# Single-bank PSUM pools for the expert products of an attention and MoE kernel

## The chip, the cores and the metric

One core of one Trainium2 chip. The metric is the device time of the program in microseconds. The kernel before took 519.79 us, the median of three runs (519.32 to 521.63).

## What is computed

Attention over q, k, v (4 batches, 8 heads, 768 positions, 64 wide), each position looking at a window of 16 and at sums of blocks of 32, gives 3072 rows x of 512. Each row then goes to one of eight experts:

```python
logits = x @ w_gate
e_idx = np.argmax(logits, axis=1)
...
for e in range(E):
    mask = e_idx == e
    ...
    h = np.maximum(x[mask] @ w1[e], 0.0)
    ye = h @ w2[e]
    out[mask] = gate_w[mask, None] * eom[mask, e, None] * ye
```

w1 is 8 x 512 x 1024, w2 is 8 x 1024 x 512, all in fp32.

## The kernel before

`body` computes the attention first, head group by head group, with the routing between. The rows of an expert are then worked off in items of up to 256 tokens, and a half item has up to 128. fp32 products are made of two halves of each operand: `split_w` (L885, L886) makes a weight's high half on ACT and its low half on DVE out of a raw tile that SP's queue loads; `take_x` (L888 to L901) transposes the gathered tokens on TensorE (L898) and splits them into xh (ACT, L900) and xl (DVE, L901).

A wide item (`full`) has eight first products (`first_wide`, L924), one for each 128 of the 1024 hidden columns: each is four pairs of matmuls (L932, L934) into one PSUM bank. Its bank is read by ACT (L936) and DVE (L937), which make lo; out of lo come hh (relu on ACT, L938) and hl (DVE, L939). The second products (`second_block`, L1115 to L1117, called Y below) multiply hh and hl with w2's halves into two banks, 48 matmuls for an item, six for each hidden tile. `write` scales the result on DVE and ACT and scatters it by an indirect DMA of POOL (L1140). `fetch` gathers the tokens of a later item (POOL, L847), `fetch_list` the rows of its list (L832). Item 1 (`full_with`) has another form of first product (`first`, twelve matmuls of 256 columns, L916 to L918); its bank is read by ACT (hh, L919) and DVE (hl, L920) themselves. During item 1 DVE also computes the routing tables of the rest (L642 to L690 and L728 to L760).

PSUM has eight banks here: tags S, PT and PV have a pair of banks each, a tile of two banks (`bank_pair`), and TR and MS one each. `Experts.bank` gives the products their banks: for S, PT and PV the first call takes one pair tile, and then its two halves go out in turn. First products alternate between PT (even) and S (odd), Y uses PV. A wait for a tile is a wait for the readers of the whole tile.

What sets the order: up to and including item 1 the order on all engines is written by hand. Items 2 to 8 (`run`) are straight code in which only POOL's order is written, and a scheduler orders PE, ACT, DVE and SP by the dependencies. After them come branches (`rest`, `pairs`, L1158): on this input three pairs of a full item and a half item run, scheduled in the same way, the half item's PE, ACT and DVE by hand. In a half item the first products are matmuls of 512 hidden columns (L1067 to L1069) into S, relu on ACT makes h (L1075), and `turn` transposes h into PT (L1080).

```python
def bank(self, tag):
    if tag not in PAIRS:
        return self.ps.tile([P, 512], F32, name="bank", tag=tag, bufs=1)
    if tag not in self.halves:
        pair = bank_pair(self.ps, tag, f"own{tag}")
        self.halves[tag] = itertools.cycle((pair[:, 0], pair[:, 1]))
    return next(self.halves[tag])
```

Of the kernel before, what the change touches and what calls it, by code (L numbers as in the profile page):

```python
# [11 lines left out]
F32 = mybir.dt.float32  # L12
# [6 lines left out]
PSUM = bass.MemoryType.PSUM  # L19
DRAM = bass.MemoryType.DRAM  # L20

B, H, S, D = 4, 8, 768, 64
P = 128
# [8 lines left out]
PAIRS = ("S", "PT", "PV")  # L32
# [137 lines left out]
def body(tc, q, k, v, w_gate, w_ogate, w1, w2, ident, cst, out):  # L170
    nc = tc.nc
    with (
        tc.tile_pool(name="const", bufs=1, side="left") as const,
        tc.tile_pool(name="ps", bufs=2, space=PSUM) as ps,
        tc.tile_pool(name="dr", bufs=1, space=DRAM) as dr,
        tc.tile_pool(name="tail", bufs=1, side="right") as st,
    ):
        id_sb = const.tile([P, P], F32, name="id_sb")
        nc.sync.dma_start(id_sb, ident)
        c_sb = const.tile([P, C_TRI], F32, name="c_sb")  # L180
        nc.gpsimd.dma_start(c_sb, cst[:, 0:C_TRI])
        wg_sb = const.tile([P, NC, 32], F32, name="wg_sb")
        nc.gpsimd.memset(wg_sb, 0.0)
        nc.gpsimd.dma_start(wg_sb[:, :, 0:E], w_gate.rearrange("(c p) e -> p c e", p=P))
        nc.gpsimd.dma_start(wg_sb[:, :, E:2 * E], w_ogate.rearrange("(c p) e -> p c e", p=P))
        x_dr = dr.tile([N, DM], F32, name="x_dr")
        l_dr = dr.tile([E * N + P, LROW], I32, name="l_dr")

        pool_a = tc.tile_pool(name="early", bufs=1, side="left")
        pool_b = tc.tile_pool(name="late", bufs=1, side="right")  # L190
        sa, sb = pool_a.__enter__(), pool_b.__enter__()
        rt = route_setup(tc, const, sa, ps, c_sb, cst, l_dr)
        moe = Experts(tc, const, ps, w1, w2, id_sb, x_dr, l_dr, rt, out)
        with tc.manual_schedule(engines=ALL):
            made = early_slots(tc, const, c_sb, rt)

            def table():
                slots = next(made)
                if slots is not None:
                    moe.add_slots(slots)  # L200

            def begin():
                pool_a.__exit__(None, None, None)
                moe.open_first(tc.tile_pool(name="moe1", bufs=2, side="left", reuse_waits="tile"))
                moe.start()

            def swap():
                pool_b.__exit__(None, None, None)
                moe.open_second(tc.tile_pool(name="moe2", bufs=2, side="right", reuse_waits="tile"))
                moe.loads = RAWS  # L210
                moe.load_ahead()

            scatters = attention(tc, const, sa, sb, st, ps, dr, q, k, v, id_sb, c_sb, wg_sb, x_dr, l_dr, rt, moe, table,
                                 begin, swap)
            counts = moe.full_with(1, scatters, rest_slots(tc, const, c_sb, rt))
        with tc.manual_schedule(engines={mybir.EngineType.Pool}):
            moe.run()
        moe.rest(counts)
        moe.close()


def bank_pair(ps, tag, name):
    return ps.tile([P, 2, 512], F32, name=name, tag=tag, bufs=1)


def shaped(bank, shape):
    b = bank[0:shape[0], 0:math.prod(shape[1:])]
    return b if len(shape) == 2 else b.rearrange("p (a n) -> p a n", n=shape[2])


def route_setup(tc, const, sa, ps, c_sb, cst, l_dr):
    nc = tc.nc
    r = {"scatters": []}
    r["ones"] = const.tile([P, P], BF16, name="ones")
    nc.vector.memset(r["ones"], 1.0)

    warm = bank_pair(ps, "S", "warm")
    for _ in range(WARM):
        nc.tensor.matmul(warm[:, 0, 0:P], lhsT=r["ones"], rhs=r["ones"], start=True, stop=True)
    r["tri"] = const.tile([P, P], BF16, name="tri")  # L240
    tri = sa.tile([P, P], F32, name="tri_f")
    nc.gpsimd.dma_start(tri, cst[:, C_TRI:C_END])
    nc.vector.tensor_copy(r["tri"], tri)

    r["base"] = const.tile([P, E], F32, name="base")
    nc.vector.tensor_copy(r["base"], c_sb[:, C_BASE:C_BASE + E])
    r["gap"] = const.tile([P, NT], F32, name="gap")
    fill = sa.tile([P, 16, LROW], I32, name="fill")
    nc.gpsimd.memset(fill, 0)
    nc.gpsimd.iota(fill[:, :, 0:1], pattern=[[1, 16]], base=NOLIST, channel_multiplier=16)  # L250
    r["fill"] = fill
    r["pair"] = const.tile([P, 2 * TB, LROW], I32, name="pair")
    nc.gpsimd.memset(r["pair"], 0)
    return r


def attention(tc, const, sa, sb, st, ps, dr, q, k, v, id_sb, c_sb, wg_sb, x_dr, l_dr, rt, moe, table, begin, swap):
# [72 lines left out]
    def gather_means(b):  # L330
        mg = banks["mg", b] = bank([P, P], f"mg{b}")
        for j in range(4):
            nc.tensor.matmul(mg[32 * j:32 * j + 32], lhsT=c_sb[:, C_SUM:C_SUM + 32],
                             rhs=MT[:, 2 * j:2 * j + 2, :].rearrange("p h d -> p (h d)"), start=True, stop=True)
# [132 lines left out]
    def turn_x(i):  # L467
        b, tok = tiles[i]
        xp = banks["xp", i] = bank([P, NC, P], f"xtr{b}{tok}")
        for c in range(NC):  # L470
            nc.tensor.transpose(xp[:, c, :], xss[i][:, 2 * c:2 * c + 2, :].rearrange("p h d -> p (h d)"), id_sb)
# [223 lines left out]
def early_slots(tc, const, c_sb, rt):  # L695

    nc = tc.nc
    base = c_sb[:, C_BASE:C_BASE + E]
    t = const.tile([P, E], F32, name="t_early")
    ti = const.tile([P, E], I32, name="ti_early")  # L700
    nc.vector.tensor_tensor(ti, rt["base"], base, ALU.subtract)
    yield
    nc.vector.tensor_scalar(ti, ti, 8, None, ALU.logical_shift_right)
    yield
    nc.vector.tensor_copy(t, ti)
    yield
    for x in slot_table_steps(tc, const, c_sb, "a", EARLY, t, base):
        if x is None:
            yield
    slots, inc, exc = x  # L710

    early = const.tile([P, E], F32, name="early")
    capped = const.tile([P, E], F32, name="capped")
    nc.vector.tensor_scalar(capped, exc, float(EARLY), None, ALU.min)
    yield
    nc.vector.scalar_tensor_tensor(early, inc, float(EARLY), capped, ALU.min, ALU.subtract)
    rt["early"] = early
    yield slots
# [50 lines left out]
class Experts:  # L769
# [3 lines left out]
    def __init__(self, tc, const, ps, w1, w2, id_sb, x_dr, l_dr, rt, out):  # L773
        self.tc, self.const, self.ps, self.w1, self.w2 = tc, const, ps, w1, w2
        self.id_sb, self.x_dr, self.l_dr, self.rt, self.out = id_sb, x_dr, l_dr, rt, out
        self.slots, self.expert, self.raw, self.lists = {}, {}, {}, {}
        self.loads, self.at = 0, [0, 0]
        self.turn = itertools.cycle(("TR", "MS"))
        self.halves = {}
        self.ring = self.fixed(const, "lst", 6, [P, 2, LROW], I32)  # L780

    def bank(self, tag):
        if tag not in PAIRS:
            return self.ps.tile([P, 512], F32, name="bank", tag=tag, bufs=1)
        if tag not in self.halves:
            pair = bank_pair(self.ps, tag, f"own{tag}")
            self.halves[tag] = itertools.cycle((pair[:, 0], pair[:, 1]))
        return next(self.halves[tag])

    def fixed(self, pool, name, n, shape, dt):  # L790
        made = []
# [25 lines left out]
    def close(self):  # L817
        self.pool2.__exit__(None, None, None)
        self.pool1.__exit__(None, None, None)
# [399 lines left out]
```

## Time and profile before

| what | value |
|---|---|
| median of 3 runs | 519.79 us (519.32 to 521.63) |
| the profiled execution | 514.76 us, span 512.9 us, mean granted clock of TensorE 0.976 |
| TensorE (PE) busy | 476.7 us, 93% of the span |
| VectorE (DVE) busy | 386.6 us, 75% |
| ScalarE (ACT) busy | 340.3 us, 66% |
| GpSimd (POOL) busy | 222.1 us, 43% |
| moved by DMA | 222 GB/s over the span |

The span is that of the instructions of the profiled execution; the rest of its time lies around them. Attention lasts to about 190 us, item 1 and the end of the item before it to 224 us, the straight items to about 390 us, the three pairs to the end. An engine's busy time is an average over these stages.

### The profile page before, as it was taken

The page shows a single profiled execution, that of the slowest core. Times are in us where ns is not written, and L with a number is a line of the kernel's source. Part 1 is how long each engine was busy: PE and PEld are TensorE (multiplying, and loading weights), DVE is VectorE, ACT ScalarE, POOL GpSimd, SP SyncE. Part 2 cuts the span into 40 slices and gives each one's busy share as a digit, 9 for nine tenths or more (in the row PEclk, how much of TensorE's full clock was granted, in tenths as well). Part 3 has the DMA queues.
Part 4 walks back from the last instruction along what each step waited for, and adds up shares of the span by engine and source line. Part 5 has one row for each costly group of instructions (what it writes and reads, how often), then busy time and mean ns, then how long its engine had stood idle before and what let it go on. Part 6 is the DMA issues. An engine that isn't in the chain of part 4 may idle for free.

```text
span 512.9 us, 12191 instructions
## 1 busy us (share of the span) xinstructions
PE 476.7 (93%) x4166; PEld 395.7 (77%) x4166; DVE 386.6 (75%) x756; ACT 340.3 (66%) x636; POOL 222.1 (43%) x235
## 2 busy tenths in 40 slices
PE   9899989989887999899999999999997999999992
PEld 9678677776666888788888888888885877877872
DVE  1977888699682687966878777777874688797795
ACT  3587755787756664566766666776763696686783
POOL 5695632635856448644224150504233315215212
PEclk9999989999897999999999999999997999999998
DMA  9999985967554699195859494866838379589380
GB/s 237 221 252 224 224 223 132 247 195 164 143 187 158 198 390 333 45 306 186 270 158 309 143 313 151 290 192 223 260 118 286 125 231 347 162 268 372 91 289 26
DMA packets 108730, 111.38 MB, mean 217 GB/s; under 512 B 42879, under 2 KB 70111, under 8 KB 108657
## 3 DMA queue, kind: packets, MB, share of 16 engines
q1 hardware_dynamic: 100496, 93.59, 61.6%
q0 software_dynamic: 8160, 16.91, 10.1%
q8 instruction: 35, 0.57, 0.5%
q14 instruction: 39, 0.31, 0.2%
HBM read 98.71 MB, written 15.15 MB: 222 GB/s over the span
## 4 chain that ended last, share of the span: by engine, by line
PE 59%; issue 15%; DVE 12%; DMA 5%; POOL 4%; ACT 3%; SPq 2%; POOLq 0%; DVEq 0%; ACTq 0%
PE ownPV L1117 7%; PE ownPV L1116 7%; PE ownPV L1115 7%; PE ownPT L932 6%; PE ownS L932 6%; PE ownPT L934 3%; PE ownS L934 3%; DMA xg<-x_dr,lst 3%; PE bank L999 3%; PE pv L449 2%; PE pt L433 2%; PE sp L399 2%; PE bank L898 2%; DVE pr L408 2%; PE ms L324 2%
## 5 line engine op out<-in xcount | busy, mean ns | idle before, releaser
L1140 POOL DMA_INDIRECT out_dram<-y,lst x27 | 32.4, 1200 | 152.2 <-DVE y L1137 148.2
L1115 PE MATMUL ownPV<-w2h,hh 128*128 128x512 f32 x216 | 85.8, 397 | 1.2 <-ACT hh L938 1.2
L1117 PE MATMUL ownPV<-w2h,hl 128*128 128x512 f32 x216 | 85.5, 396 | 0.8 <-DVE hl L939 0.8
L1116 PE MATMUL ownPV<-w2l,hh 128*128 128x512 f32 x216 | 84.7, 392 | 0.0
L421 POOL TENSOR_TENSOR pr<-pr,mn 128x960 f32<-128x960 f32 x24 | 44.5, 1861 | 40.6 <-DVE mn L416 26.1
L886 DVE TENSOR_TENSOR w2l<-wrawb,w2h 128x512 fp32r<-128x512 f32 x80 | 53.7, 688 | 9.6 <-ACT w2h L885 9.2
L932 PE MATMUL ownPT<-xhl,w1h 128*128 128x512 f32 x160 | 59.6, 404 | 0.9 <-issue 0.9
L932 PE MATMUL ownS<-xhl,w1h 128*128 128x512 f32 x160 | 60.0, 406 | 0.0
L885 ACT ACTIVATE w2h<-wrawb 128x512 fp32r<-128x512 f32 x80 | 48.6, 630 | 11.5 <-PE ownPV L1117 11.0
L847 POOL DMA_INDIRECT xg<-x_dr,lst x34 | 37.9, 1115 | 39.6 <-PE bank L898 11.9
L886 DVE TENSOR_TENSOR w1l<-wrawb,w1h 128x512 fp32r<-128x512 f32 x77 | 50.6, 693 | 3.5 <-ACT w1h L885 2.6
L1117 PEld LDWEIGHTS ownPV<-w2h,hl 128*128 128x128 f32 x216 | 40.6, 188 | 10.0 <-DVE hl L939 1.2
L1115 PEld LDWEIGHTS ownPV<-w2h,hh 128*128 128x128 f32 x216 | 40.6, 188 | 10.0 <-ACT hh L938 1.7
L938 ACT ACTIVATE hh<-lo 128x256 fp32r<-128x256 f32 x80 | 32.4, 412 | 23.3 <-DVE lo L937 18.8
L885 ACT ACTIVATE w1h<-wrawb 128x512 fp32r<-128x512 f32 x80 | 46.1, 622 | 0.3
L939 DVE SCALAR_TENSOR_TENSOR hl<-lo,hh 128x256 fp32r<-128x256 f32 x80 | 33.3, 422 | 16.8 <-ACT hh L938 16.8
L1116 PEld LDWEIGHTS ownPV<-w2l,hh 128*128 128x128 f32 x216 | 40.6, 188 | 6.3
L934 PE MATMUL ownS<-xhl,w1l 128*128 128x256 f32 x160 | 45.4, 284 | 0.0
L934 PE MATMUL ownPT<-xhl,w1l 128*128 128x256 f32 x160 | 45.3, 283 | 0.0
L832 POOL DMA_INDIRECT lst<-l_dr,rowib x30 | 33.9, 1131 | 12.5 <-issue 9.5
L886 DVE TENSOR_TENSOR w2l<-wrawa,w2h 128x512 fp32r<-128x512 f32 x48 | 32.2, 688 | 8.1 <-ACT w2h L885 7.9
L932 PEld LDWEIGHTS ownPT<-xhl,w1h 128*128 128x128 f32 x160 | 30.6, 191 | 8.5 <-issue 1.5
(220 smaller groups left out, 1102.6 us busy)
## 6 DMA issues: line engine op xcount, KB each, us to landing
wrawb<-in_moe_w_dram SPq DMA_DIRECT2D x160, 256.0 KB, 5.0
wrawa<-in_moe_w_dram SPq DMA_DIRECT2D x88, 256.0 KB, 4.9
raw_k<-in_k_dram SPq DMA_DIRECT2D x12, 512.0 KB, 8.2
raw_q<-in_q_dram SPq DMA_DIRECT2D x12, 512.0 KB
vw<-in_v_dram SPq DMA_DIRECT2D x44, 128.0 KB, 5.0
x_dr<-xs SPq DMA_DIRECT2D x14, 256.0 KB, 2.0
x_dr<-xs POOLq DMA_DIRECT2D x10, 256.0 KB, 4.7
vw<-in_v_dram SPq DMA_DIRECT2D x33, 64.0 KB, 4.4
```

The lines of the kernel that those rows point to most:

```text
L421: nc.gpsimd.tensor_tensor(pr, pr, mns.pop(i).unsqueeze(2).to_broadcast([P, H, W]), ALU.subtract)
L832: i = nc.gpsimd.indirect_dma_start(out=lst[:, t, :], out_offset=None, in_=self.l_dr, in_offset=bass.IndirectOffsetOnAxis(ap=self.slots[s][ ...
L847: nc.gpsimd.indirect_dma_start(out=self.xg[t], out_offset=None, in_=self.x_dr[0:rows, :], in_offset=bass.IndirectOffsetOnAxis(ap=self.list ...
L885: nc.scalar.activation(hi, raw, AF.Copy)
L886: (lo_by or nc.vector).tensor_tensor(lo, raw, hi.bitcast(F32), ALU.subtract)
L932: nc.tensor.matmul(hp.rearrange("p a n -> p (a n)"), lhsT=w_h[:, fs], rhs=self.x[:, c].rearrange("p a n -> p (a n)"), start=c == 0, stop=F ...
L934: nc.tensor.matmul(hp[:, 1, :], lhsT=w_l[:, fs], rhs=self.xh[:, c, :], start=False, stop=c == NC - 1)
L938: nc.scalar.activation(hh[:, j, :], lo, AF.Relu)
L939: nc.vector.scalar_tensor_tensor(hl[:, j, :], lo, 0.0, hh[:, j, :].bitcast(F32), ALU.max, ALU.subtract)
L1115: nc.tensor.matmul(y, lhsT=hh[:, j, tk], rhs=w_h, start=j == 0, stop=False)
L1116: nc.tensor.matmul(y, lhsT=hh[:, j, tk], rhs=w_l, start=False, stop=False)
L1117: nc.tensor.matmul(y, lhsT=hl[:, j, tk], rhs=w_h, start=False, stop=j == NF - 1)
```

## The change

The pool of PSUM becomes three pools: TR and MS, S and PT, PV. They are opened as before, and `bank_pair` goes on taking pairs from them. At the first expert product that asks for S or PT, and at the first that asks for PV, the pool of that tag is closed and opened again, and from then on `Experts.bank` takes a new tile of one bank for each product, two buffers a tag (`reuse_waits="tile"`: a tile taken from the reopened pool waits for the tiles that held its bytes before, not for the whole old pool).

```diff
--- before.py
+++ after.py
@@ -171,10 +171,10 @@
     nc = tc.nc
     with (
         tc.tile_pool(name="const", bufs=1, side="left") as const,
-        tc.tile_pool(name="ps", bufs=2, space=PSUM) as ps,
         tc.tile_pool(name="dr", bufs=1, space=DRAM) as dr,
         tc.tile_pool(name="tail", bufs=1, side="right") as st,
     ):
+        ps = Banks(tc)
         id_sb = const.tile([P, P], F32, name="id_sb")
         nc.sync.dma_start(id_sb, ident)
         c_sb = const.tile([P, C_TRI], F32, name="c_sb")
@@ -217,6 +217,37 @@
             moe.run()
         moe.rest(counts)
         moe.close()
+        ps.close()
+
+
+class Banks:
+
+    def __init__(self, tc):
+        self.tc = tc
+        self.single = {}
+        self.pools = {"TR MS": self.open("TR MS", "left"), "S PT": self.open("S PT", "left"),
+                      "PV": self.open("PV", "right")}
+
+    def open(self, tags, side, **more):
+        pool = self.tc.tile_pool(name="ps_" + tags.replace(" ", ""), bufs=1, space=PSUM, side=side, **more)
+        return pool, pool.__enter__()
+
+    def of(self, tag):
+        return next(x for x in self.pools if tag in x.split())
+
+    def tile(self, shape, dtype, name, tag, bufs):
+        return self.pools[self.of(tag)][1].tile(shape, dtype, name=name, tag=tag, bufs=bufs)
+
+    def part(self, tag):
+        tags = self.of(tag)
+        if tags not in self.single:
+            self.pools[tags][0].__exit__(None, None, None)
+            self.pools[tags] = self.open(tags, "right" if tags == "PV" else "left", reuse_waits="tile")
+            self.single[tags] = True
+
+    def close(self):
+        for tags in ("PV", "S PT", "TR MS"):
+            self.pools[tags][0].__exit__(None, None, None)
 
 
 def bank_pair(ps, tag, name):
@@ -776,16 +807,12 @@
         self.slots, self.expert, self.raw, self.lists = {}, {}, {}, {}
         self.loads, self.at = 0, [0, 0]
         self.turn = itertools.cycle(("TR", "MS"))
-        self.halves = {}
         self.ring = self.fixed(const, "lst", 6, [P, 2, LROW], I32)
 
     def bank(self, tag):
-        if tag not in PAIRS:
-            return self.ps.tile([P, 512], F32, name="bank", tag=tag, bufs=1)
-        if tag not in self.halves:
-            pair = bank_pair(self.ps, tag, f"own{tag}")
-            self.halves[tag] = itertools.cycle((pair[:, 0], pair[:, 1]))
-        return next(self.halves[tag])
+        if tag in PAIRS:
+            self.ps.part(tag)
+        return self.ps.tile([P, 512], F32, name="bank", tag=tag, bufs=2 if tag in PAIRS else 1)
 
     def fixed(self, pool, name, n, shape, dt):
         made = []
```

Lines above 810 move by 31 where they stand behind the new class, those behind the changed `bank` by 27: L916 becomes L943, L898 becomes L925, L932 becomes L959, L1115 to L1117 become L1142 to L1144, L1080 becomes L1107.

The instructions up to the end of item 1 stand in the same order on every engine. On PE, in item 1, where product 2 (twelve matmuls) ends and product 3 begins, before (ownPT and ownS are the pair tiles):

```order
L916 MATMUL ownPT_3123<-xhl_3013,w1h3_2429 128x256
L917 MATMUL ownPT_3123<-xhl_3013,w1h3_2429 128x256
L918 MATMUL ownPT_3123<-xhl_3013,w1l3_2920 128x256
L916 MATMUL ownS_3159<-xhl_3013,w1h0_2426 128x256 [waits DVE_49]
L917 MATMUL ownS_3159<-xhl_3013,w1h0_2426 128x256
L918 MATMUL ownS_3159<-xhl_3013,w1l0_2871 128x256
L916 MATMUL ownS_3159<-xhl_3013,w1h1_2427 128x256
```

and now (each bank_n is a tile of one bank):

```order
L943 MATMUL bank_3196<-xhl_3024,w1h3_2435 128x256
L944 MATMUL bank_3196<-xhl_3024,w1h3_2435 128x256
L945 MATMUL bank_3196<-xhl_3024,w1l3_2926 128x256
L943 MATMUL bank_3217<-xhl_3024,w1h0_2432 128x256
L944 MATMUL bank_3217<-xhl_3024,w1h0_2432 128x256
L945 MATMUL bank_3217<-xhl_3024,w1l0_2877 128x256
L943 MATMUL bank_3217<-xhl_3024,w1h1_2433 128x256
```

Product 3 no longer waits for DVE. Products 1 to 3 begin without a wait, products 4 to 7 still wait for DVE, for readers of the bank four products back.

On PE, at the end of the last straight item, the end of its last first product and what follows, before:

```order
L932 MATMUL ownS<-xhl,w1h_2432 128x512
L934 MATMUL ownS<-xhl,w1l_2950 128x256
L932 MATMUL ownS<-xhl,w1h_2433 128x512
L934 MATMUL ownS<-xhl,w1l_2978 128x256
L1115 MATMUL ownPV<-w2h_2761,hh 128x512 [waits Activation_49]
L1116 MATMUL ownPV<-w2l_2765,hh 128x512
L1117 MATMUL ownPV<-w2h_2761,hl 128x512 [waits DVE_49]
L1115 MATMUL ownPV<-w2h_2761,hh 128x512
```

and now:

```order
L959 MATMUL bank<-xhl,w1h_2438 128x512
L961 MATMUL bank<-xhl,w1l_2956 128x256
L959 MATMUL bank<-xhl,w1h_2439 128x512
L961 MATMUL bank<-xhl,w1l_2989 128x256
L1144 MATMUL bank<-w2h_2459,hl 128x512
L1142 MATMUL bank<-w2h_2459,hh 128x512
L1143 MATMUL bank<-w2l_2463,hh 128x512
L1144 MATMUL bank<-w2h_2459,hl 128x512
```

Each shows the last rows of the item's eighth first product. Before, eighteen Y matmuls follow it up to the branch, the first of them waiting for ACT and DVE; now forty follow it, and those shown belong to an early hidden tile.

On PE, in each pair, the transposes of the half item's tokens (L898, L925), before:

```order
L932 MATMUL ownS<-xhl,w1h_2428 128x512
L934 MATMUL ownS<-xhl,w1l_2916 128x256
L932 MATMUL ownS<-xhl,w1h_2429 128x512
L934 MATMUL ownS<-xhl,w1l_2920 128x256
L898 MATMUL bank<-id_sb,xg_2442 128x128 [waits DMASW6_49,PE_49]
L898 MATMUL bank<-id_sb,xg_2442 128x128 x3
L932 MATMUL ownPT<-xhl,w1h_2426 128x512 [waits DVE_49]
L934 MATMUL ownPT<-xhl,w1l_2871 128x256
```

and now:

```order
L1142 MATMUL bank<-w2h_2461,hh 128x512 [waits Activation_49]
L1143 MATMUL bank<-w2l_2465,hh 128x512
L1144 MATMUL bank<-w2h_2461,hl 128x512 [waits DVE_49]
L1142 MATMUL bank<-w2h_2461,hh 128x512
L1143 MATMUL bank<-w2l_2465,hh 128x512
L1144 MATMUL bank<-w2h_2461,hl 128x512
L925 MATMUL bank<-id_sb,xg_2448 128x128 [waits DMASW6_49]
L925 MATMUL bank<-id_sb,xg_2448 128x128 x3
L1142 MATMUL bank<-w2h_2766,hh 128x512 [waits Activation_49]
```

Before, they follow two first products of the pair's wide item; now they follow all eight and some twenty Y matmuls.

## Rows read from the trace of the kernel before

**Rows 1.** Stage windows: us, busy time of PE, PEld, DVE, ACT, POOL, PEclk, DMA share, GB/s
```profile
193.00:229.00 36.00, 32.77 (x208) 28.77 (x207) 28.49 (x93) 18.15 (x38) 23.66 (x34) 1.00 0.66 223
...
262.00:385.00 123.00, 123.00 (x637) 104.39 (x635) 95.81 (x186) 85.43 (x187) 35.54 (x30) 1.00 0.66 213
385.00:423.00 38.00, 34.90 (x157) 27.89 (x156) 26.28 (x49) 24.20 (x50) 11.03 (x10) 0.91 0.67 212
```

**Rows 2.** Waits of PE: engine, line, releaser, total us, times, longest
```profile
PE ownPT L916 <- DVE dab L660: 2.5, 1, 2.5
PE bank L898 <- DMA xg<-x_dr,lst: 2.2, 2, 1.2
...
PE ownPV L1115 <- ACT hh L938: 1.2, 1, 1.2
...
PE ownPV L1117 <- DVE hl L939: 0.8, 1, 0.8
```

**Rows 3.** Timeline of PE, item 1: start us, duration us, instruction, [idle before]
```profile
196.95 0.28 PE L916 MATMUL ownPT<-xhl,w1h 128*128 128x256 f32 x1
...
202.16 0.38 PE L916 MATMUL ownS<-xhl,w1h 128*128 128x256 f32 x1 [0.73 <-DVE hl L920]
...
203.69 0.28 PE L916 MATMUL ownPT<-xhl,w1h 128*128 128x256 f32 x1
...
205.13 0.28 PE L916 MATMUL ownS<-xhl,w1h 128*128 128x256 f32 x1
...
209.22 0.39 PE L916 MATMUL ownPT<-xhl,w1h 128*128 128x256 f32 x1 [2.49 <-DVE dab L660]
...
212.33 0.40 PE L1115 MATMUL ownPV<-w2h,hh 128*128 128x512 f32 x1
...
224.17 0.40 PE L932 MATMUL ownPT<-xhl,w1h 128*128 128x512 f32 x1
```

**Rows 4.** Timeline of DVE, item 1
```profile
204.31 0.42 DVE L920 SCALAR_TENSOR_TENSOR hl<-ownS,hh 128x256 fp32r<-128x256 f32 x1 [1.17 <-ACT hh L919]
...
208.75 0.42 DVE L920 SCALAR_TENSOR_TENSOR hl<-ownPT,hh 128x256 fp32r<-128x256 f32 x1
...
219.53 1.28 DVE L901 TENSOR_TENSOR xhl<-bank,xhl 128x512 fp32r<-128x512 f32 x2
```

**Rows 5.** Timeline of PE, end of the straight items and first pair
```profile
386.55 0.50 PE L1115 MATMUL ownPV<-w2h,hh 128*128 128x512 f32 x1 [1.22 <-ACT hh L938]
...
390.37 0.79 PE L932 MATMUL ownPT<-xhl,w1h 128*128 128x512 f32 x1 [0.94 <-issue]
...
395.65 0.69 PE L898 MATMUL bank<-id_sb,xg 128*128 128x128 f32 x4
...
399.66 0.39 PE L932 MATMUL ownS<-xhl,w1h 128*128 128x512 f32 x1
...
400.01 0.39 PE L932 MATMUL ownS<-xhl,w1h 128*128 128x512 f32 x1
```

**Rows 6.** Windows around the first branch, columns as in rows 1
```profile
390.00:392.00 2.00, 1.63 (x5) 1.45 (x6) 0.82 (x2) 0.78 (x2) 1.22 (x1) 0.50 0.93 334
...
396.00:398.00 2.00, 2.00 (x14) 1.78 (x12) 0.85 (x2) 0.86 (x3) 1.54 (x2) 1.00 0.17 55
```

**Rows 7.** Timeline of PE, second and third pair
```profile
432.83 0.63 PE L898 MATMUL bank<-id_sb,xg 128*128 128x128 f32 x4 [0.97 <-DMA xg<-x_dr,lst]
...
470.18 0.63 PE L898 MATMUL bank<-id_sb,xg 128*128 128x128 f32 x4 [1.22 <-DMA xg<-x_dr,lst]
```

**Rows 8.** Timeline of PE, first half item
```profile
416.97 0.39 PE L1068 MATMUL ownS<-w1l,xhl 128*128 128x512 f32 x1
417.20 0.39 PE L1069 MATMUL ownS<-w1h,xhl 128*128 128x512 f32 x1
```

**Rows 9.** Timeline of ACT, first half item
```profile
417.62 0.60 ACT L1075 ACTIVATE h<-ownS 128x512 f32<-128x512 f32 x1
```

**Rows 10.** Costliest groups of the page: busy us, mean ns, idle before
```profile
L886 DVE TENSOR_TENSOR w2l<-wrawb,w2h 128x512 fp32r<-128x512 f32 x80 | 53.7, 688 | 9.6 <-ACT w2h L885 9.2
```

## The prediction

> **What bounds the kernel now.** I read the stage windows first. TensorE (PE) is busy for 123.00 of 123 us from 262 to 385, in the straight wide items, at a granted clock of 1.00 [rows 1]: nothing that only shortens a wait can gain there. In the stages beside it PE stands still for part of the time: 36.00 - 32.77 = 3.2 us between 193 and 229 (item 1), and 3.1 us between 385 and 423, where the clock is 0.91 too. Second, the waits of PE name these pauses [rows 2]: expert products of item 1 that wait for DVE (L916, 2.5 us), X transposes that wait for the gather of tokens (L898, 2.2 us in two waits), and two Y products at the end of the last straight item (L1115, 1.2 us and L1117, 0.8 us). Third, PE's own timeline shows where each pause stands [rows 3, 5, 7], and DVE's what it did meanwhile [rows 4].
>
> **The change, part by part.** Until the first expert product on S or PT nothing moves. From there a product's bank is a tile of its own, so it waits for the readers of that bank alone, four products back; before, the two halves of a pair were one tile, and it waited for the readers of the other half as well, two products back.
>
> *Item 1 (A).* The order is written by hand and stays; only waits go. The eight products run from 196.95 to 212.33, 15.38 us [rows 3]. Product 3 starts at 202.16 after a wait, just as the hl of product 1 has ended, and product 6 starts at 209.22, just as the hl of product 4 ends (208.75 + 0.42 = 209.17 [rows 4]); the bank that product 6 writes had been read out long before. The routing arithmetic stands ahead of that hl on DVE, so the wait is long. Product 4 ran without a wait, from 203.69 to 205.13, 1.44 us for its twelve matmuls; eight of these make 11.5, so 3.9 us go. The rows of the order show products 1 to 3 without a wait on DVE, and products 4 to 7 with one that has long been met. Is it given back? Item 2's products began at 224.17 and would at 220.3. They need the token halves that DVE finishes at 219.53 + 1.28 = 220.81. DVE works without a break from the hl of product 3 (204.31) on; that hl comes 0.62 us after its product's end (203.69), and now the product ends at 196.95 + 4 x 1.44 = 202.7, so DVE starts about 1.0 us earlier and the halves are there at 219.8. That is 0.5 us before PE wants them. I take A = 3.9; the lower bound, if DVE's chain moves by nothing or a little, is 0.9.
>
> *Straight items 2 to 8.* The scheduler issues three or four first products in a row where Y products stood between them, and collects some forty Y matmuls at the item's end. PE was full here, the matmuls are the same, so this is costed at nothing. What covers it: with four products in a row (4 x 1.40 us, from pairs that follow each other by 0.35 [rows 5]) a bank is wanted again 5.6 us after its product began; the product takes 1.4, and its release needs one 128x256 step on ACT and one on DVE (0.42 us each, like the hl of [rows 4]), which leaves 3.4 us for other work ahead of them in those queues. If the cover goes, the second rival prices it.
>
> *The end of the last straight item (B, C).* Before, the last first product ended 18 Y matmuls before the branch, and the Y matmuls of its own hidden tile waited 1.2 and 0.8 us for hh and hl [rows 2, 5]. Now some forty Y matmuls follow it; at 0.23 each, as the 128x512 matmuls of [rows 8] are, that is 9 us against a chain of four steps. B = 2.0. [...] A pause of 0.97 and one of 1.22 elsewhere [rows 7] are followed by product steps at full pace, and the 3.2 us of pauses in item 1 left its stage at 1.00 [rows 1]; so I take C = 2.5, with zero as the lower end.
>
> *The pairs (D).* In three pairs the transposes of the half item stood right behind two products and waited for their gather, 0.97 and 1.22 us in the second and third pair [rows 7]. In the new order they stand behind all eight products and some twenty Y matmuls: 6 x 1.4 + 24 x 0.23 = 14 us later, so both waits go: D = 2.2. POOL's order changes with it: the second gather now follows the two list fetches and waits for those later transposes. Its tokens are wanted only in the next item's turn, more than 10 us on, and a gather's wait here was about a microsecond; costed at nothing, for up to 1 us if it comes late. In the half items the transposes of h now follow relu's product after 6 matmuls instead of 12. From that product's last matmul (417.20) to the end of relu (417.62 + 0.60) are 1.0 us [rows 8, 9], and 6 x 0.23 is 1.4. With one more ACT step ahead of relu this is a stall of up to 0.3, three times, and as much for the second turn: I subtract 0.6 (between 0 and 1.8).
>
> Sum: 3.9 + 2.0 + 2.5 + 2.2 - 0.6 = **10.0 us**. The profiled execution, 514.76, would become 504.8. The runs shown have a median of 519.79, 5.0 above it; the pauses are of the program, not of one run, so I subtract from the median: **509.8**.
>
> [...] The straight stage gains nothing in my sum because PE has no pause there [rows 1]. [...]
>
> **The rivals.** *Less (a chance of 0.18, 515.3 us).* DVE's chain holds item 2, so that A is 0.9, and the branch's pause alone still brings the half clock, so that C is 0: 0.9 + 2.0 + 2.2 - 0.6 = 4.5. For it: DVE has no idle time between 204.65 and 220 but for what product 3 gave it, and my margin is 0.5 us; against it: DVE's splits of weights in that stretch are ahead of need.
>
> *Slower (0.05, 525 us or so).* Bursts of products ask ACT and DVE for their releases in a burst. The mechanism sits in the ten wide items (seven straight, three in pairs): a weight split, 0.69 us on DVE [rows 10] and about as long on ACT, delays a release that stands behind it, and five of them in the two queues use up the 3.4 us. One product held up by 1.5 us per item costs 15 and leaves +5. It decides from 1.26 us per item, (10.0 + 2.6) / 10. For it: both engines do 16 such splits per item. Against it: the Y matmuls at an item's end give them 9 us in which nothing waits.
>
> *No change (0.05, 519.8).* The scheduler keeps every wait, because the last reader of a tile, and not of a bank, would still be waited for. Against it: the rows of the order show the waits gone in item 1.
>
> *The clock (0.04, 519.8).* PE now goes through four banks instead of two halves; short pauses between groups of matmuls let the clock fall more often. A fall as at 390 costs 2.5 us, so four of them undo the gain. Against it: pauses in item 1 and in the pairs left it at 1.00. [...] The straight stage, which went round its banks at 1.00 for 123 us, doesn't bear it out.
>
> **How the numbers follow.** The forecast has 0.68, its own range 506 to 512: the upper end is C at half and stalls at 1.8, the lower one has no stalls and lets 3 of the 5.0 us between profiled and timed runs be pauses of the kind that go. With "less" this is 0.86 for faster by over 0.5% (2.6 us, about what a measurement of this kernel can tell from no change). No change and the clock make 0.09, slower 0.05. The range reaches to 516.5, past the price of "less", and leaves out the other rivals and a little below.
>
> **What would show it.** A: no wait of an L916 product (L943 there) over 0.3 us, and item 2's products at 220 to 220.5. B and C: no pause at the last Y matmuls, and a clock of 1.00 in every window between 385 and 400. D: no X transposes that wait for the gather. Straight items: PE still at its full share, each as long as before. Wrong would be: item 2 at 223 (DVE), a half clock after the branch (C), waits of L959 products for lo, or of L1107 transposes for h, above 1 us in total.

## The result and the profile after

The changed kernel takes 503.62 us (median of 4 runs, 502.72 to 504.70), the kernel before 519.56 us (4 runs, 516.69 to 521.63): a ratio of 0.970, with an interval of 0.965 to 0.975. That is 15.9 us, where 10.0 were forecast; 503.62 lies below the range. The profiled execution of the changed kernel took 504.70 us, its span 502.8.

The stage windows of the changed kernel (columns as in [rows 1]):

```profile
193.00:229.00 36.00, 36.00 (x229) 31.93 (x228) 32.26 (x99) 20.72 (x41) 26.17 (x36) 1.00 0.68 243
...
262.00:385.00 123.00, 123.00 (x637) 104.57 (x636) 96.06 (x188) 85.48 (x187) 34.67 (x32) 1.00 0.70 227
385.00:423.00 38.00, 38.00 (x193) 31.71 (x192) 30.41 (x56) 28.50 (x59) 13.96 (x12) 1.00 0.79 262
```

TensorE now works without a pause in each of them, at a clock of 1.00; before, 3.2 us of the first and 3.1 us of the last were pauses [rows 1]. The waits of PE (as in [rows 2]):

```profile
PE pt L464 <- ACT pr L456: 11.8, 2, 11.4
PE sp L430 <- DVE pr L439: 1.6, 1, 1.6
```

No wait of an expert product is left, and none of the transposes for a gather. All that remain stand in attention and its routing. The largest is the wait that L433 had before, 6.1 us then, nearly twice as long in this execution; attention's instructions stand in the same order in both, and e9 and e14 below ask whether the change has a part in it.

Where the time went is read best from the first instructions of the stages on PE (as in [rows 3, 5]; L1144 is a Y matmul, the last line is the last one):

```profile
201.37 0.28 PE L943 MATMUL bank<-xhl,w1h 128*128 128x256 f32 x1
...
224.71 0.40 PE L959 MATMUL bank<-xhl,w1h 128*128 128x512 f32 x1
...
386.06 0.62 PE L1144 MATMUL bank<-w2h,hl 128*128 128x512 f32 x2
386.51 0.40 PE L959 MATMUL bank<-xhl,w1h 128*128 128x512 f32 x1
...
493.24 0.40 PE L1144 MATMUL bank<-w2h,hl 128*128 128x512 f32 x1
```

| stage | before, us | after, us | difference | forecast |
|---|---|---|---|---|
| start of item 1 | 196.95 | 201.37 | +4.4 | 0 |
| item 1, to the first product of item 2 | 27.2 | 23.3 | -3.9 | -3.9 |
| straight items, to the first product behind the branch | 166.2 | 161.8 | -4.4 | -2.0 |
| pairs, to the last second product | 112.8 | 106.7 | -6.1 | -4.1 |

(The last Y product before stood at 503.16.) The three stages that the change touches give back 14.4 us; attention, whose instructions it leaves as they were, ended 4.4 us later in this execution.

### The profile page after: what moved, and what is told of

Its sections match the earlier page's. It is cut to its first block, busy times and chain, and to the rows that moved or that the text cites. A ratio compares the mean times of both kernels' runs of the same rounds, so it can differ in the third digit from the quotient of the medians.

```text
span 502.8 us, 12203 instructions
## 1 busy us (share of the span) xinstructions
PE 469.4 (93%) x4166; PEld 392.4 (78%) x4166; DVE 386.8 (77%) x756; ACT 338.4 (67%) x636; POOL 218.6 (43%) x235
## 4 chain that ended last, share of the span: by engine, by line
PE 77%; DVE 11%; DMA 3%; issue 3%; ACT 2%; POOL 2%; SPq 1%; DVEq 0%; POOLq 0%; ACTq 0%
PE bank L959 15%; PE bank L1142 10%; PE bank L1144 10%; PE bank L1143 10%; PE bank L961 8%; PE bank L1026 3%; PE pt L464 3%; DVE pr L439 3%; PE pv L480 2%; PE sp L430 2%; PE ms L355 2%; PE bank L925 2%; DVE mn L447 2%; DMA raw_k<-in_k_dram 2%; DVE vw L303 1%
## 5 line engine op out<-in xcount | busy, mean ns | idle before, releaser
L959 PE MATMUL bank<-xhl,w1h 128*128 128x512 f32 x320 | 114.5, 397 | 0.0
L961 PE MATMUL bank<-xhl,w1l 128*128 128x256 f32 x320 | 89.3, 280 | 0.0
L1142 PE MATMUL bank<-w2h,hh 128*128 128x512 f32 x216 | 86.5, 401 | 0.0
L1143 PE MATMUL bank<-w2l,hh 128*128 128x512 f32 x216 | 84.4, 391 | 0.0
L1144 PE MATMUL bank<-w2h,hl 128*128 128x512 f32 x216 | 83.1, 394 | 0.0
L959 PEld LDWEIGHTS bank<-xhl,w1h 128*128 128x128 f32 x320 | 60.0, 188 | 13.5
L961 PEld LDWEIGHTS bank<-xhl,w1l 128*128 128x128 f32 x320 | 60.4, 189 | 1.8
L1144 PEld LDWEIGHTS bank<-w2h,hl 128*128 128x128 f32 x216 | 40.5, 188 | 9.5 <-DVE hl L1110 0.8
L1143 PEld LDWEIGHTS bank<-w2l,hh 128*128 128x128 f32 x216 | 40.6, 188 | 7.9
L1142 PEld LDWEIGHTS bank<-w2h,hh 128*128 128x128 f32 x216 | 40.6, 188 | 7.8
L464 PE MATMUL pt<-id_sb,pr 128*120 128x128 f32 x192 | 28.7, 290 | 13.1 <-ACT pr L456 11.8
L964 DVE TENSOR_TENSOR lo<-bank,lo 128x256 f32<-128x256 f32 x80 | 32.5, 419 | 7.2 <-ACT lo L963 5.2
```

The costliest lines, as they stand in the source:

```text
L464: nc.tensor.transpose(pt[0:W, x, hp, :], prs[i][:, x, hp, :], id_sb)
L959: nc.tensor.matmul(hp.rearrange("p a n -> p (a n)"), lhsT=w_h[:, fs], rhs=self.x[:, c].rearrange("p a n -> p (a n)"), start=c == 0, stop=F ...
L961: nc.tensor.matmul(hp[:, 1, :], lhsT=w_l[:, fs], rhs=self.xh[:, c, :], start=False, stop=c == NC - 1)
L964: nc.vector.tensor_tensor(lo, hp[:, 0, :], lo, ALU.add)
L1142: nc.tensor.matmul(y, lhsT=hh[:, j, tk], rhs=w_h, start=j == 0, stop=False)
L1143: nc.tensor.matmul(y, lhsT=hh[:, j, tk], rhs=w_l, start=False, stop=False)
```

## The experiments

The three stage lengths of the table are read from each profile. They are far steadier than the times: the straight items of the changed kernel and of the kernels that share their code took 161.63 to 162.12 us in eight profiles, those in which a first product waits for the readers of the one two back (five with pair tiles, and e7) 165.9 to 166.4 in six. The runs came in four groups. In the second the kernel before took 519.2 us, as it had; in the first, third and fourth 527.0, 528.7 and 526.1. There, PE shows short pauses with the releaser "issue" (PE waited for nothing that the profile shows) in attention and in item 1:

```profile
221.04 0.28 PE L943 MATMUL bank<-xhl,w1h 128*128 128x256 f32 x1 [0.96 <-issue]
222.49 0.36 PE L943 MATMUL bank<-xhl,w1h 128*128 128x256 f32 x1 [0.93 <-issue]
```

(the timeline of PE in e9, item 1). The first comparison and the second group have none in item 1 and at most one in attention. The granted clock falls in item 1 too: it is 0.90 in e9 from 208 to 241, where it was 1.00 in the changed kernel's first profile. Of the 9.1 us that item 1 is longer in e9 (32.5 against 23.3), 4.6 are such pauses. So item 1 is compared within a group; straight items and pairs don't show the difference.

**e1 to e3: the change by stage.** A mode in `Experts.bank` gives pair tiles or single banks; in e1 it is "single" up to item 1, in e2 "pair" up to item 1, in e3 "pair" in the straight items alone.

```diff
     def bank(self, tag):
+        if tag in PAIRS and self.mode == "pair":
+            if tag not in self.halves:
+                pair = self.ps.pair(tag)
+                self.halves[tag] = itertools.cycle((pair[:, 0], pair[:, 1]))
+            return next(self.halves[tag])
         if tag in PAIRS:
             self.ps.part(tag)
```

e1:

> Single banks in item 1 only; items 2 and on take halves of pair tiles again. Three stage lengths of the profile are read: item 1 (its first product to the first product of item 2; 27.2 us before, 23.3 after), straight items (to the first product behind the branch; 166.2 and 161.8), pairs (to the last second product; 112.8 and 106.6). Theory (each pause was cured where it stood): 23.3, about 166, 112.8, in all 3.9 us less than before, 515.6. Rival (VectorE's table chain or a later stage gives item 1's gain back): straight items longer by 2 to 4 us and the time as before, 519.5.

Measured: item 1 32.0 us, straight items 166.4, pairs 112.3; 524.98 us, a ratio of 0.997 (0.993 to 1.000), so the time alone shows 1.7 us (0 to 3.5) and not the 3.9. Item 1 with pair tiles took 34.3 and 35.5 us in the same group (e2, e4), so its gain was 2.3 to 3.5 here; the clock over item 1 was 0.90 in e1 and e2 and 0.86 in e4, so the 2.3 is the fairer figure. The later stages gave none of it back: they are as before, not 2 to 4 us longer. The rival falls.

e2:

> The reverse: pair tiles up to the end of item 1, single banks from item 2 on. Theory: item 1 27.2, straight items 161.8, pairs 106.6, in all 10.5 us less than before, 509. Rival (later stages gained because item 1 handed over earlier): straight items or pairs longer than 161.8 and 106.6 by over 1 us, 511 or more.

Measured: 161.80 and 106.70 us; 516.37 us, a ratio of 0.979 (0.973 to 0.986), 10.6 us less than before. The later stages gain all of theirs without item 1.

e3:

> Single banks in item 1 and in the branches, pair tiles in the straight items 2 to 8. Theory (the pauses at the end of the last straight item drag the pause at the branch and the half clock behind them): item 1 23.3, straight items about 166, pairs 106.6 + 2.5 = 109.1 with a clock of 0.50 behind the branch, in all 507 to 512. Rival (the half clock comes from the pair-wide waits of the products behind the branch): pairs 106.6 and a clock of 1.00 there.

Measured: straight items 166.4, pairs 108.75; 519.97 us, a ratio of 0.985 (0.978 to 0.991). The kernel's PE timeline and clock windows at the branch:

```profile
396.18 0.50 PE L1159 MATMUL ownPV<-w2h,hh 128*128 128x512 f32 x1 [1.22 <-ACT hh L982]
...
397.73 0.80 PE L1161 MATMUL ownPV<-w2h,hl 128*128 128x512 f32 x1 [0.81 <-DVE hl L983]
...
400.00 0.79 PE L976 MATMUL bank<-xhl,w1h 128*128 128x512 f32 x1 [0.20 <-PE ownPV L1161]
```

```profile
397.00:399.00 2.00, 1.27 (x3) 1.08 (x4) 0.67 (x2) 0.00 (x0) 0.00 (x0) 0.64 0.79 230
399.00:401.00 2.00, 1.80 (x5) 1.00 (x5) 1.16 (x2) 1.00 (x2) 0.13 (x1) 0.50 0.94 341
...
405.00:407.00 2.00, 2.00 (x13) 1.72 (x12) 0.88 (x3) 1.25 (x4) 1.59 (x2) 1.00 0.28 99
```

The products behind the branch have single banks and run at the low clock all the same, so the rival falls. The clock was down before the branch: the mean of 0.64 from 397 to 399 and a pause of only 0.20 at the first product say so. That leaves the two pauses ahead of the branch, as the theory has it (e7 takes one of them nearly away). The low clock costs the pairs 108.75 - 106.7 = 2.05 us.

**e4: the transposes alone.** The kernel before, with an ordering edge from the last first product to the half item's transposes:

```diff
-                self.take_x(nxt_n)
+                self.take_x(nxt_n, late=nxt_n == 1)
...
+                    if late:
+                        self.tc.add_manual_dep(i.ins, self.last_f, mybir.DependencyInfo(
+                            mybir.DependencyClass.NoSync, mybir.DependencyReason.DATA))
```

> The kernel before with one thing moved: in the pairs, the four transposes of the half item's tokens stand behind the last first product. Theory (order, not banks, cured the wait for the gather): pairs 112.8 - 2.5 = 110.3, no transposes that wait for the gather, the other stages as before, 517. Rival (a later transpose delays the half item as much): pairs 112 to 113 and a new wait at the half item's first products.

```profile
407.81 0.65 PE L935 MATMUL ownPT<-xhl,w1h 128*128 128x512 f32 x1 [1.06 <-issue]
...
412.25 0.40 PE L935 MATMUL ownPT<-xhl,w1h 128*128 128x512 f32 x1
...
448.60 0.50 PE L935 MATMUL ownPT<-xhl,w1h 128*128 128x512 f32 x1 [0.60 <-DVE w2l L886]
...
485.10 0.51 PE L935 MATMUL ownPT<-xhl,w1h 128*128 128x512 f32 x1 [0.59 <-issue]
```

Measured: pairs 110.0 us, straight items 165.9; 523.27 us, a ratio of 0.994 (0.990 to 0.998). No transposes wait for the gather; two other pauses of 0.60 and 0.59 us came at first products. The theory holds: the place of the transposes, not the form of the banks, cured this wait, and the single banks gave it by the order that they allowed. But not all of the 2.8 us by which the pairs are shorter belong to it: the first eight pairs of product steps take 412.25 - 407.81 = 4.44 us here and 5.28 in the kernel before, because the clock is back earlier. About 2.0 us are left for the new order, with its two new pauses in it.

**e5 and e6: which banks.** In e5 only S and PT get single banks, in e6 only PV (the condition in `bank` above becomes a test of the tag).

> Single banks for the first products (S and PT) alone; the second products keep the two halves of one pair tile. Theory (all of the gain is in the first products' waits): item 1 23.3, straight items 161.8, pairs 106.6, 503.6 as the changed kernel. Rival (second products waited for the scaling of both output banks): longer by over 1 us in straight items or pairs.

Measured: 23.34, 162.1 and 106.5 us; 506.16 us, a ratio of 0.974 (0.967 to 0.981). All of it is in the first products.

> Single banks for the second products (PV) alone. Theory: item 1 27.2, straight items 166, pairs 112.8, 519.5 as before. Rival: shorter by over 1 us somewhere.

Measured: 28.6, 166.1 and 110.7; 518.42 us, a ratio of 0.999 (0.994 to 1.003). The time is as before. Pairs are 2.1 us shorter, which the theory did not have and the rival had without a place or a reason; e7 shows why. Item 1 is 1.4 us longer than the 27.2 forecast: its two waits are those of the kernel before (0.73 and 2.51 us), but the clock over it is 0.94, where it was 1.00 before.

**e7: depth or form.**

```diff
-        return self.ps.tile([P, 512], F32, name="bank", tag=tag, bufs=2 if tag in PAIRS else 1)
+        return self.ps.tile([P, 512], F32, name="bank", tag=tag, bufs=2 if tag == "PV" else 1)
```

> The changed kernel with one buffer for S and one for PT in place of two each: a product waits for the bank of the product two back, two of the four banks lie idle. Theory (what was gained is the distance of four products): as before in every stage, 27.2, 166, 112.8, 519.5. Rival (a tile of its own and a reopened pool are what helps): 23.3, 162, 107, 503.6.

Measured: 27.24, 166.05 and 109.9 us; 517.59 us, a ratio of 0.998 (0.994 to 1.001). Item 1 has its two waits back, 0.74 and 2.50 us, and the straight items are as before. A tile for each product and a pool opened anew do nothing by themselves; the distance to the product whose readers are waited for does it. The pairs are the surprise. At their start:

```profile
390.29 0.51 PE L1142 MATMUL bank<-w2h,hh 128*128 128x512 f32 x1 [1.23 <-ACT hh L965]
...
391.81 0.73 PE L1144 MATMUL bank<-w2h,hl 128*128 128x512 f32 x2 [0.32 <-DVE hl L966]
394.07 0.49 PE L959 MATMUL bank<-xhl,w1h 128*128 128x512 f32 x1 [1.52 <-issue]
```

```profile
391.07:393.07 2.00, 1.16 (x4) 0.30 (x2) 1.41 (x3) 0.48 (x1) 0.00 (x0) 1.00 0.71 198
393.07:395.07 2.00, 1.00 (x5) 0.91 (x6) 0.73 (x2) 0.72 (x2) 1.38 (x2) 1.00 0.80 268
395.07:397.07 2.00, 2.00 (x14) 1.76 (x13) 0.42 (x1) 0.55 (x2) 1.27 (x2) 1.00 1.03 389
```

The scheduler put two Y matmuls between the waiting ones, so the second pause is 0.32 instead of 0.81, and the clock stays at 1.00, though pauses of 1.23, 0.32 and 1.52 us stand within 5 us (e6 has 1.22, 0.34 and 1.53 and a clock of 1.00 too). That is the 2 to 3 us of the pairs.

**e8, e10 and e13: the branch.** In the changed kernel's profile nothing is left of the pause of 0.94 at the branch: 0.45 us lie between the start of the last two Y matmuls and the first product (above). A waiting transpose in front of the branch should bring it back:

```diff
             self.full(s)
+        xp = shaped(self.bank("TR"), [P, P])
+        self.tc.nc.tensor.transpose(xp, self.last_y[:, 0:P], self.id_sb)
```

> The changed kernel with one transpose of 128x128 more, between the last second product of the straight items and the branch, which waits for the scaled output of that product; nothing reads its result. It puts a pause of 1.2 us on TensorE there. Theory (a pause ahead of the branch exposes the branch's own 0.94 and, with it, lowers the clock): straight items 161.8 + 1.2 + 0.9 = 164, and pairs 106.6 + 2.5 = 109 with a clock of 0.50 in the first windows, 508. Rival (each stands by itself): 163.1 and 106.6, 505.

Measured: straight items 165.0, pairs 106.66; 509.59 us, a ratio to before of 0.982 (0.974 to 0.990). The timeline:

```profile
389.06 0.33 PE L1179 MATMUL bank<-id_sb,y 128*128 128x128 f32 x1 [0.78 <-ACT y L1166]
391.30 0.49 PE L959 MATMUL bank<-xhl,w1h 128*128 128x512 f32 x1 [1.92 <-issue]
```

The pause at the branch is back, longer than before, and the clock did not fall: half of the theory holds. From the end of the wait to the first product behind the branch are 2.24 us. The same distance, from the last Y that waited, is 390.37 - 388.09 = 2.28 in the kernel before, and 2.26, 2.27, 2.25, 2.27 and 2.26 in e1, e3, e4, e6 and e7, with one to four matmuls in between (the waiting one included), at either clock. So the time counts from the last wait. In the trace of the kernel before, PE's sequencer (PEldq there) begins the first of four loads of the counts at 388.1, with the Y that waited, and ends the second of two branches at 390.3. In the changed kernel the same six stand from 383.0 to 385.2, beside Y matmuls that follow each other without a pause up to the first product at 386.51. e10 puts 32 more transposes behind the waiting one:

> As the kernel with the pause ahead of the branch, and 32 more transposes of 128x128 behind the waiting one (about 0.09 us each, 2.9 in all), which wait for nothing; nothing reads them. Theory (the branch's 2.25 us count from the end of the last wait, and matmuls that wait for nothing hide them): straight items 161.8 + 0.8 + 2.9 = 165.5, no pause at the first product behind the branch. Rival (the branch costs its own time after the last matmul): 165.5 + 1.9 = 167.4.

```profile
402.19 0.33 PE L1179 MATMUL bank<-id_sb,y 128*128 128x128 f32 x1 [0.78 <-ACT y L1166]
402.36 3.66 PE L1181 MATMUL bank<-id_sb,y 128*128 128x128 f32 x32
407.17 0.49 PE L959 MATMUL bank<-xhl,w1h 128*128 128x512 f32 x1 [1.16 <-issue]
```

Measured: straight items 167.7; 522.27 us, a ratio of 0.989 (0.986 to 0.992). Both expectations miss: a pause is left, but of 1.16 us, not 1.9, and the transposes took 0.11 us each, not 0.09. If the first load of the counts stood 2.25 us ahead of the first product here too, it began at 407.17 - 2.25 = 404.9, with some ten transposes still to run; this is an estimate. e13 asks the same with longer matmuls:

> The changed kernel with the waiting transpose ahead of the branch and, behind it, 14 matmuls of 256 columns in fp32 (0.23 us each, 3.2 in all) in place of the 32 short transposes; nothing reads them. Theory (the sequencer reaches the branch some ten matmuls ahead of the array, so that 2.25 us hide behind ten matmuls of 0.23, and only half behind ten of 0.11): no pause at the first product behind the branch, straight items 161.8 + 0.8 + 0.2 + 3.2 = 166.0. Rival (1.2 us of the branch can never hide behind work that follows a wait): 167.2.

```profile
397.59 0.33 PE L1179 MATMUL bank<-id_sb,y 128*128 128x128 f32 x1 [0.78 <-ACT y L1166]
397.75 6.21 PE L1181 MATMUL bank<-y 128*128 128x256 f32 x28
403.61 0.58 PE L959 MATMUL bank<-xhl,w1h 128*128 128x512 f32 x1
```

Measured: no pause; 521.83 us in the one run. The 14 fp32 matmuls stand in the trace as 28 of 0.21, so the straight items were 168.8 us and not 166.0, but the question is answered: 28 matmuls of 0.21 us behind the wait hid the branch. The ten matmuls ahead are an estimate from e10 alone; in the changed kernel fifteen Y were still to start at the first load of the counts, at 383.0, and five when the second branch ended, at 385.2.

**e9, e14, e11, e12, e15: attention's part.** e9 and e14 are the changed kernel again. In e11 one step of the order by hand moves (`fr.0`, GpSimd's gather for item 0, behind `su.21`), in e12 and e15 further, behind `su.22` ("the kernel before" in the text of e12 is e11's):

```diff
-... lt.7:T fr.0 lt.8:M su.21 ma.22 ...
+... lt.7:T lt.8:M su.21 fr.0 ma.22 ...
```

> The changed kernel once more, beside the next three on the same chip. Theory: straight items 161.8, pairs 106.6 us as in its first profile whatever the chip; the start of item 1 (201.4 in that profile, 196.9 in that of before) varies by several us, since attention's wait for GpSimd, not the change, sets it. Rival (the change made attention's end later): start of item 1 at 201 or later in every profile of it, and 197 in those of pair-tile kernels.

> The changed kernel once more: straight items 161.8 and pairs 106.7 whatever the chip; start of item 1 anywhere from 197 to 208.

Measured: straight items 161.80 in both, pairs 106.70 and 106.72; start of item 1 208.3 and 201.8; 516.48 us, a ratio of 0.977 (0.975 to 0.980), and 516.32 us, 0.981 (0.975 to 0.987). Kernels in which item 1's products wait two back started it at 201.65, 206.42, 202.62 and 200.78 (e2, e4, e6, e7), so the change is hardly to blame, and the rival, as it was put, falls. Of these only e4 is built on the kernel before; the others have the three pools. The medians say the same. What a median leaves beside the three stage lengths is 519.56 - 306.2 = 213.4 us before and 503.62 - 291.9 = 211.7 after; in the second group it is 519.16 - 306.2 = 213.0 before, and 213.0 to 214.6 in e5 to e8. The 196.95 of the kernel before is the earliest of all 17 profiles.

> The changed kernel with one step of the order by hand moved in attention: GpSimd's gather of item 0's tokens stands behind the subtraction of head group 21 instead of ahead of it. Theory (that gather waits for its list, and three subtractions behind it hold up ScalarE and TensorE): the pause of 11.4 us shorter by 4 to 6, 498 to 500. Rival (the gather then comes late for item 0's transposes): a new wait there of the same size, 503.

> As the kernel before, with the gather behind the subtraction of head group 22, so two of them (3.5 us) stand in the time in which the gather waited for its list. Theory: the pause shorter by 6 to 8 us, 496 to 499. Rival: item 0's transposes wait for the gather, no better than with one subtraction.

> The kernel with the gather of item 0's tokens behind the subtraction of head group 22, once more. Theory: where the pause of attention is long (11 us), 5 us or more less than the changed kernel on the same chip; where it is 3 us, the same as the changed kernel. Rival: the same as the changed kernel on any chip.

Measured: 517.80, 516.62 and 514.47 us, ratios of 0.981, 0.978 and 0.978 (0.972 to 0.983), beside 0.977 and 0.981 of the changed kernel in the same groups: no difference. All three fell into groups where the wait of L464 is 3 to 4 us; it went, and item 0's transposes waited 2.7 to 3.0 us for the gather in its place, as the rival has it. Where that wait is 11 us, the second and better test, it was not tried.

## Why the prediction came out too small

**Item 1 (A) held to the tenth.** Forecast 3.9; 27.2 - 23.3 = 3.9. Item 2 was forecast 23.35 us after the start of item 1 and came after 23.34. The token halves were ready at 222.81 + 1.28 = 224.09, 0.6 us before PE's 224.71 (the forecast had 0.5):

```profile
222.81 1.28 DVE L928 TENSOR_TENSOR xhl<-bank,xhl 128x512 fp32r<-128x512 f32 x2
```

So DVE's chain did not hold item 2, and "less" did not happen here.

**Straight items: right.** PE's 123.00 of 123 us stayed, the burst of first products held up none of them, and "slower" had nothing to feed on. No wait of an expert product is left, against "no change".

**The end of the straight items (B) was too small: it priced the two waits and left the pause of 0.94 us at the branch [rows 5] in place.** I took that pause as the branch's own. It is what is left of 2.25 us after the last wait, and in the changed kernel no wait stands near the end, so it hid behind Y matmuls. The steps of PE before (from the start of one matmul to the start of the next; 386.55 and 390.37 stand in [rows 5]) show what went:

```profile
384.93 0.40 PE L1117 MATMUL ownPV<-w2h,hl 128*128 128x512 f32 x1
...
386.88 0.40 PE L1116 MATMUL ownPV<-w2l,hh 128*128 128x512 f32 x1
388.09 0.50 PE L1117 MATMUL ownPV<-w2h,hl 128*128 128x512 f32 x1 [0.81 <-DVE hl L939]
388.43 0.40 PE L1115 MATMUL ownPV<-w2h,hh 128*128 128x512 f32 x1
...
388.90 0.53 PE L1117 MATMUL ownPV<-w2h,hl 128*128 128x512 f32 x1
```

The two pauses are 2.4 us, as steps of 1.62 and 1.21 in place of 0.23; the branch is 1.2, a step of 1.47 in place of 0.23; the matmul after each of the two waits had a step of 0.34, 0.2 together. That is 3.8 of the 4.4, where I had 2.0. The other 0.6 lies in the transposes of tokens: the step behind the first matmul after a group of them is 0.08 longer in both kernels, and the straight items have 13 such groups before and 9 after, 0.3 us; and two steps between transposes were slow before, 0.25.

**The clock (C) went as forecast,** 2 to 3 us against 2.5: by e3 it is 2.05, by e7 at most 2.9 (of which 0.5 are shorter waits for the gather). The 2.5 is what the first eight pairs of product steps behind the branch lost before: 5.28 us, at a clock of 0.50 from 389.0 to 395, in place of 2.8. The pause at the branch was no part of the cause before:

```profile
388.00:389.00 1.00, 0.91 (x4) 0.67 (x4) 0.04 (x1) 0.00 (x0) 0.00 (x0) 1.00 1.07 221
389.00:390.00 1.00, 0.43 (x2) 0.00 (x0) 0.53 (x1) 0.54 (x1) 0.00 (x0) 0.50 0.98 254
```

The clock fell at 389.0, and that pause lies from 389.43 to 390.37. But the reason was too simple: I argued from pauses that had not lowered the clock, and e7 and e8 show more pause time in one stretch (1.23 + 0.32 + 1.52 and 0.78 + 1.92 us) at a clock of 1.00. Nor do like pauses always end alike: item 1's 0.73 and 2.5 us left it at 1.00 in the kernel before and in e7, and in e6 a low stretch followed them. The sum was right; which pattern of pauses lowers the clock stays open.

**The pairs (D) were right, the 0.6 for the half items was not.** As steps the two waits of the transposes were 1.24 and 1.50 us in place of 0.12, together 2.5, against 2.2. The stalls that I subtracted did not come: no transposes of h waited. Instead the half items' own matmuls start faster: before, one of PE's steps from a Y to a first product of the half item was 0.52 us in each, now 0.23. The pairs' 6.1 us are 2.5 (C: 5.28 us for the first eight pairs of product steps, now 2.8), 2.5 (D), and 0.9 of such starts, and 0.2 that I didn't follow. The starts came back to 0.23 in e4 too, with pair tiles, so they hang on the order; no run was made for them alone.

**The rest is the way from the profile to the median.** The stages give 14.4 us, the medians 15.9. I saw that the profiled execution stood 5.0 us below the median and let only a part of that into the range. It had the earliest start of item 1 of 17 profiles, 4 to 11 us ahead of the others. A sum against that execution would have given 504.8, close to the 504.70 of the new profile, but by two errors that cancel. In the groups with the "issue" pauses the changed kernel gained 12.2 and 9.8 us, so part of the difference between 10 and 16 is the group in which a kernel is measured, and the interval of 0.965 to 0.975 doesn't cover that.

## What to carry to other kernels

Look at what a wait names: if a product waits for the reader of a buffer that it doesn't write, smaller tiles are worth a try, and the gain can be read beforehand from the stage lengths (here 3.9 forecast, 3.9 measured). The cured waits took with them what stood in their shadow: the branch behind them (1.2 us), the low clock (2.05 us by e3), the first slow matmul after each (0.2 together); price those as zero only with a reason. And compare stages, not whole runs, when a stage that the change doesn't touch varies by more than the change is worth.

## What the runs showed of the hardware

From the last wait on TensorE to the first matmul behind the first branch (two nested conditions and four loads of the counts stand there) it took 2.24 to 2.28 us in seven kernels, whatever few matmuls lay in between; with 28 matmuls of 0.21 us behind the waiting one no pause was left (e13), with 32 of 0.11 us 1.16 (e10). In the changed kernel, where no wait stood near, the loads and branches lay from 383.0 to 385.2 beside Y matmuls, and there was no pause. The granted clock fell to 0.50 after pauses of 1.22 and 0.81 us (before, e3), and stayed at 1.00 through 1.23, 0.32 and 1.52 (e7). After the same two waits of item 1 (0.73 and 2.5 us) it stayed at 1.00 before and in e7 and fell for some 3 us in e6 (a mean of 0.94 over item 1). In three of four groups of runs the same code showed pauses marked "issue" in attention and item 1, mostly of up to 1.1 us (one of 1.66 in e4, one of 3.19 in e2), and a clock of 0.86 to 0.90 over item 1 (e1, e2, e4, e9); the kernel before took 7 to 9.5 us longer there than in the second group. What makes the pauses is open; the second and the fourth group ran on the chip with the same number, so the chip alone is not it.
